# Windowed and global attention feeding a two-layer network: another order of the global columns, the stores and the value products

## The chip, the cores and the metric

The kernel runs on one core of a Trainium2 chip. The metric is the device time of one execution in microseconds (us), median of several runs. A core has five instruction streams that run side by side and meet only at semaphores: TensorE (PE in the profile, with its weight loads as PEld), VectorE (DVE), ScalarE (ACT), GpSimd (POOL) and SyncE (SP), which here only issues DMAs. Each stream executes its instructions in the order in which they stand.

## The reference

For 8 batches and 8 heads of width 64 there are 512 local and 32 global positions. Global queries attend to all 544 positions. Local queries attend to the 32 global keys and to local keys at most 32 positions away. The attention output (4352 rows of 512) then goes through a gated network with 2048 inner columns.

```python
s_g = scale * q_g @ concat(k_g, k_l).T ;  out_g = softmax(s_g) @ concat(v_g, v_l)
s_l = concat(scale * q_l @ k_g.T, where(|i - j| <= 32, scale * q_l @ k_l.T, -1e9))
out_l = softmax(s_l) @ concat(v_g, v_l)
x = concat(out_g, out_l) as rows of 512     # 8 * 544 rows
h = x @ w_in                                # 512 x 2048
out = (h * sigmoid(h)) @ w_out              # 2048 x 512
```

All inputs and the output are float32. The network's products, and from step 28 on the score products, are made out of rounded parts: a value is split into a high part (a cast) and a low part (value minus high part), and a product is a sum of high and low terms.

## The kernel before

**Attention steps.** Work is cut into 128 steps; step k is one batch, one chunk of 128 local queries and one pair of heads, so a batch has 16 steps. A step goes through these functions:

- `st_load` (L295) brings queries and keys, `st_vload` (L303) the values; both DMAs are issued by SP. `st_split` (L311) makes high and low parts for steps from `ND` = 28 on: a ScalarE cast (L317) and two VectorE subtractions (L318, L319).
- `st_scores` (L321): PE products into a PSUM bank `s` (L336), then the softmax: mask and minimum on VectorE (L340), exponential on ScalarE (L344), scaling (L348, L349). The result is `probs`, two buffers.
- For steps from `KF` = 16 on the probabilities are turned by DMA: `st_halves` (L359) copies them on POOL into 16-bit halves, `st_away` (L364) writes these to DRAM, `st_back` (L368) reads them back with a transposing DMA into the tile `pt`. There are three `pt` tiles, used in turn. Steps before 16 are turned by PE (L377).
- `st_turn` (L371) adds the columns of the global queries of the same batch to `pt`: a POOL copy from `pgt` (L386) and, in the last chunk of a batch, one from `pgu` (L389).
- `st_out` (L391): the value products (L403) into a PSUM bank `o`, evacuated to the network's input by ScalarE (L405) and VectorE (L407), with the global part added to `acc` (L413).

**Global steps.** In the course of batch b the global queries of batch b + 1 are prepared, at four steps of the batch, the heads of the stream: `g_load` (L217), `g_split` (L222), `g_scores` (L233), which makes two products `gs`, each evacuated by ScalarE (L247 or L251) and, for batches from 3 on, VectorE (L252), and, after two of them, `g_soft`. The names `gs_4_1` and the like give batch and head pair. The first of the two products goes to a bank of kind `s`, the second to kind `o`. Once the first network block is done, `attbank` (L80) has one single bank for everything of kind `o`, so that a value product that follows a `gs` product has to wait until the `gs` product has been read out. `g_turn` (L273), at the start of a batch, turns the global probabilities and writes `pgt` and `pgu`.

**The network.** It runs in 12 blocks of row tiles (`SIZES`: one tile, then eleven blocks of three). Block n has 16 pairs of `first_layer` (L538: 12 products `h` at L551, then ScalarE L557, VectorE L559, ScalarE L563, VectorE L564) and `second_layer` (L567: for each of three tiles the products L579, L580, L581 into banks `out`). At the end of a block each `out` is evacuated by ScalarE (L590) into one of two buffers and stored by a DMA (L592). In blocks 2 to 10 that DMA keeps its place in program order on SP (`hold`). The weights' high and low parts are made once, in blocks 0 and 1, by `split_weights` (L204): ScalarE casts (L211), POOL subtractions (L212).

**What sets the order.** Attention and network share PE. Every function of a step is put into one list with a due time: a step takes one unit, and each head widens its step by 0.3. The tables `DUE`, `DMAT` (for steps from 16 on), `HEAD` and `TURN` hold the due times relative to the step's start. The list is sorted, and `fill` (L524) emits what is due between two pieces of the network. PE executes exactly in this order. The other engines' order is chosen by a scheduler, except where `hold` keeps program order.

Of the kernel before, what the change touches and what calls it, by code (L numbers as in the profile page):

```python
# [38 lines left out]
SIZES = (1,) + (3,) * 11  # L39
BUFS = dict(qk=2, raw=2, p=2, vraw=4, halves=1, pt=3)  # L40
ND = 28
KF = 16
# [1 line left out]
KP = 12  # L44
SCRATCH = 8
FETCH, LOOK = 4, 2
SPLIT0, SPLITS = 14, 1.0
FIRSTW = {0: 2, 1: 1, 2: 1, 3: 2}

FIRST = dict(load=(-1.2, -1.1, -1.0, 0.1), vload=(-0.9, 0.2, 0.3, 1.1), turn=(3.2, 4.0, 4.9, 5.8), out=(4.3, 5.2, 6.1, 7.0),  # L50
# [1 line left out]
             join=(3.9, 5.0, 5.9, 6.8), late=8.5, then=7.3)  # L52

DUE = dict(load=-1.2, split=-0.5, vload=-0.6, turn=1.6, out=2.2)
DMAT = dict(vload=1.5, halves=0.7, away=1.05, back=1.7, turn=2.3, out=3.0)
HEAD = dict(load=-0.2, split=0.45, scores=0.65, soft=0.85, slot=0.3)
HEADS0, HEADS = (10, 1), (7, 2)
TURN = (1.5, 2.6)
FULL = 0.98
END = 0.5  # L60

# [1 line left out]
def attention_moe_kernel(ctx: ExitStack, tc: tile.TileContext, qk0_in, qk_in, v_in, gqk, wts, out):  # L63
    nc = tc.nc
# [69 lines left out]
    def pt_tile(k):  # L134
        return pts[k % len(pts)]
# [30 lines left out]
    hold = tc.keep_in_program_order  # L166
# [90 lines left out]
    def did(what, *needs):  # L257
        for need in needs:
            assert need in order_done, (what, need)
        order_done.add(what)  # L260
# [32 lines left out]
    tiles = {}  # L293
# [70 lines left out]
        hold(nc.sync.dma_start(out=away, in_=tiles.pop(("halves", k)).rearrange("p h u j -> p h (u j)")))  # L364

    def st_back(k, b, c, pr):
        pt = tiles["pt", k] = pt_tile(k)
        hold(nc.sync.dma_start_transpose(out=pt.bitcast(U16).rearrange("p u a q -> p (u a) q")[:, :, : 2 * P],  # L368
                                         in_=tiles.pop(("away", k)).rearrange("q h j -> (q h) j")))

    def st_turn(k, b, c, pr):  # L371
        if k < KF:
            t = attbank("t", f"t{k}")
            p = tiles.pop(("p", k))
            assert k in held_by.values()
            for i in range(4):
                nc.tensor.transpose(t[:, i * P : (i + 1) * P], p[:, i * P : (i + 1) * P], ident.bitcast(F32))  # L377
            pt = tiles["pt", k] = pt_tile(k)
            nc.scalar.copy(out=pt[:, :, :, :P], in_=t.rearrange("p (u a q) -> p u a q", u=2, a=2))
        else:  # L380
            pt = tiles["pt", k]
        if k < NPR:
            return
        did(("last", b) if (c, pr) == (NC - 1, NPR - 1) else k, ("turn", b, pr // 2))
        pgt, pgu = state["pgt"]
        nc.gpsimd.tensor_copy(out=pt[:, :, 0, P:], in_=pgt[:, c, 2 * pr : 2 * pr + 2, :])  # L386
        if c == NC - 1:
            src = pgu[SG * pr : SG * (pr + 1), :].rearrange("p (u q) -> p u q", u=2)
            nc.gpsimd.tensor_copy(out=pt[:SG, :, 1, P:], in_=src)  # L389
# [65 lines left out]
    at = 0.0  # L455

    def put(when, fn, *a):
        stream.append((when, fn, a))

    AHEAD = NPR  # L460
    for k, (t, b, c, pr) in enumerate(steps):
        a = (k, b, c, pr)
        j = k % NST
        due = dict(DUE)
        if k >= KF:
            due.update(DMAT)
        if k < AHEAD:
            due.update({part: FIRST[part][k] - k for part in ("load", "vload", "turn", "out")})
        if k == AHEAD:
            for h in range(NPR):  # L470
                put(FIRST["gload"][h], g_load, 0, h)
                put(FIRST["gscores"][h], g_scores, 0, h)
                put(FIRST["join"][h], join_weights)
            for hh in range(2):
                put(FIRST["gsoft"][hh], g_soft, 0, hh)
                put(FIRST["gturn"][hh], g_turn, 0, hh)
            put(FIRST["late"], g_late)
            at = FIRST["then"]
        if j == 0 and b:
            for hh in range(2):  # L480
                put(at + TURN[hh], g_turn, b, hh)
        for i in range(FIRSTW.get(k, 0)):
            put(at + 0.01, fetch_weights, nc.sync)
        put(at + due["load"], st_load, *a)
        put(at + due["split"], st_split, *a)
        put(at, st_scores, *a)
        put(at + due["vload"], st_vload, *a)
        if k >= KF:
            put(at + due["halves"], st_halves, *a)
            put(at + due["away"], st_away, *a)  # L490
            put(at + due["back"], st_back, *a)
        put(at + due["turn"], st_turn, *a)
        put(at + due["out"], st_out, *a, t)
        marks[t] = at + due["out"]
        if j == NST - 1 and b % 4 == 3:
            put(marks[t] + 0.001, g_tile, t + 1)
            marks[t + 1] = marks[t] + 0.001
        if b + 1 < B:
            for h in [h for h in range(NPR) if int((HEADS if b else HEADS0)[0] + h * (HEADS if b else HEADS0)[1]) == j]:
                for part, fn in (("load", g_load), ("split", g_split), ("scores", g_scores)):  # L500
                    put(at + HEAD[part], fn, b + 1, h)
                if h % 2:
                    put(at + HEAD["soft"], g_soft, b + 1, h // 2)
                at += HEAD["slot"]
        at += 1.0
# [61 lines left out]
    def second_layer(n, f, gh, gl):  # L567
        if f == 0:
            outs[n] = [ps_out.tile([P, DM], F32, tag=f"out{i}", name=f"out{n}_{i}") for i in range(SIZES[n])]
        wh, wl = (w_hi[f][:, DM:], w_lo[f][:, DM:]) if n else (w_32[2 * f + 1], None)  # L570

        last = n + 1 == len(SIZES) and f == NF - 1
        for i in (reversed(range(SIZES[n])) if last else range(SIZES[n])):
            o = outs[n][i]
            sl = slice(i * P, (i + 1) * P)
            if n == 0:
                nc.tensor.matmul(o, gh[:, sl], wh, start=(f == 0), stop=(f == NF - 1))
            else:
                nc.tensor.matmul(o, gh[:, sl], wh, start=(f == 0), stop=False)  # L579
                nc.tensor.matmul(o, gh[:, sl], wl, start=False, stop=False)  # L580
                nc.tensor.matmul(o, gl[:, sl], wh, start=False, stop=(f == NF - 1))  # L581
            fill(1)
        if f == NF - 1:
            for i in (reversed(range(SIZES[n])) if last else range(SIZES[n])):
                o = outs[n][i]
                if last and i == 0:
                    sb = raws.tile([P, QW + KW], F32, tag="raw", name="o_last")[:, :DM]
                else:
                    sb = two.tile([P, DM], F32, tag="o", name=f"o{n}_{i}")
                nc.scalar.activation(sb, o, AF.Copy, scale=0.5)  # L590
                for p0, np_, r in out_rows(sum(SIZES[:n]) + i):
                    store = nc.sync.dma_start(out=out[r : r + np_, :], in_=sb[p0 : p0 + np_, :])  # L592
                    if 1 < n < len(SIZES) - 1:
                        hold(store)

    advance(ends[0])
    early.clear()
# [1 line left out]
    for n in range(len(SIZES)):  # L599
        for f in range(NF):  # L600
# [13 lines left out]
            if pend is not None:  # L614
                second_layer(*pend)
            pend = (n, f, *g)
    second_layer(*pend)


# [67 lines left out]
```

## Time and profile before

| quantity | value |
|---|---|
| three runs | 1060.27, 1054.97, 1062.12 us; median 1060.27 us |
| profiled execution | 1055.09 us, span from first to last instruction 1053.3 us |
| mean granted TensorE clock | 0.986 of full speed |
| PE busy, of the span | 996.9 us (95%) |
| DVE, ACT, POOL busy | 612.0, 577.9, 233.1 us |
| DMA issues by SP | 112 transposing DMAs `pt<-away`, 40 stores, and the loads |

In a row of the profile, `L403 PE MATMUL o<-pt,vraw` is line, engine, operation, and what is written from what is read, buffer numbers left out. Behind a group of instructions stand busy time and mean nanoseconds of one, then the idle time of the engine just before them with what ended it. In a timeline a row is start, duration, engine and line; in square brackets stands the idle time before it and what ended that. "issue" means that the profile shows no releaser. A PE instruction's end is modelled, and matmuls overlap, so their pace is read from their starts. PEclk is the TensorE clock that was granted.

### The profile page before, as it was taken

The numbers are of one execution on the slowest core, as the hardware profiler recorded it, in microseconds if no ns is written. First come the engines' busy times: TensorE is split into PE (matmuls) and PEld (weight loads), VectorE is DVE, ScalarE is ACT, GpSimd is POOL, SyncE is SP. The second block draws the span as 40 slices with busy tenths as digits, with TensorE's granted clock in tenths as the row PEclk, the third lists the DMA queues.
The fourth block names the chain that finished last, engine by engine and source line by source line (L and its number), as shares of the span: only waits on it lengthen the run. The fifth ranks groups of instructions, "written<-read, shape, count | busy, mean of one in ns | idle before, by whom it ended". The sixth has DMA issues, their size and how long they took to land.

```text
span 1053.3 us, 17559 instructions
## 1 busy us (share of the span) xinstructions
PE 996.9 (95%) x5680; PEld 847.1 (80%) x5680; DVE 612.0 (58%) x1941; ACT 577.9 (55%) x1517; POOL 233.1 (22%) x437
## 2 busy tenths in 40 slices
PE   7898998999989998999998999899989999999997
PEld 5666886888878887888887887788778888888996
DVE  4777544656676666665556665665566657552222
ACT  6687665655555555564455556556555656542322
POOL 2003765222222212211112222112212222110000
PEclk8899999999999999999999999999999999999999
DMA  8795454556565665555446556555645656630000
GB/s 301 273 349 177 116 146 112 157 150 168 143 181 144 156 178 143 148 144 139 118 119 146 145 152 179 140 152 151 172 135 141 163 155 160 165 92 26 30 1 30
DMA packets 185562, 155.23 MB, mean 147 GB/s; under 512 B 125824, under 2 KB 145792, under 8 KB 185472
## 3 DMA queue, kind: packets, MB, share of 16 engines
q1 hardware_dynamic: 181728, 140.49, 48.9%
q10 hardware_dynamic: 3744, 13.63, 3.6%
q8 instruction: 45, 0.74, 0.3%
q14 instruction: 45, 0.37, 0.1%
HBM read 86.44 MB, written 38.27 MB: 118 GB/s over the span
## 4 chain that ended last, share of the span: by engine, by line
PE 79%; DMA 7%; ACT 4%; DVE 4%; issue 3%; POOL 2%; SPq 0%; ACTq 0%; POOLq 0%; DVEq 0%
PE h L551 31%; PE out L579 11%; PE out L581 10%; PE out L580 10%; PE o L403 7%; PE s L336 6%; DMA raw_g<-in_gqk_dram 2%; ACT probs L344 2%; DMA raw<-in_qk_dram 2%; DMA pt<-away 1%; POOL halves L359 1%; DMA away<-halves 1%; PE h L545 1%; DMA vraw<-in_v_dram 1%; PE gs L246 1%
## 5 line engine op out<-in xcount | busy, mean ns | idle before, releaser
L359 POOL COPY halves<-probs 128x512 uint16<-128x512 uint16 x224 | 145.0, 670 | 487.2 <-DVE probs L349 303.1
L551 PE MATMUL h<-xh,w_hi 128*128 128x384 f32 x704 | 239.9, 341 | 0.0
L551 PE MATMUL h<-xh,w_lo 128*128 128x384 f32 x704 | 237.3, 337 | 0.7 <-POOL w_lo L212 0.7
L551 PE MATMUL h<-xl,w_hi 128*128 128x384 f32 x704 | 236.6, 336 | 0.0
L579 PE MATMUL out<-w_hi,gh 128*128 128x512 f32 x528 | 216.1, 409 | 0.7 <-ACT o L590 0.7
L581 PE MATMUL out<-w_hi,gl 128*128 128x512 f32 x528 | 209.7, 397 | 0.6 <-DVE gl L564 0.6
L580 PE MATMUL out<-w_lo,gh 128*128 128x512 f32 x528 | 209.1, 396 | 0.0
L557 ACT ACTIVATE t<-h 128x384 f32<-128x384 f32 (+1 forms) x192 | 90.2, 470 | 192.8 <-PE h L551 189.6
L559 DVE SCALAR_TENSOR_TENSOR t<-t,h 128x384 f32<-128x384 f32 x176 | 97.3, 553 | 149.0 <-ACT t L557 147.3
L344 ACT ACTIVATE probs<-probs,st 128x224 f32<-128x224 f32 x244 | 115.9, 476 | 78.0 <-DVE st L340 76.8
L564 DVE TENSOR_TENSOR gl<-t,gh 128x384 fp32r<-128x384 f32 x176 | 104.9, 596 | 74.4 <-PE out L581 63.6
L551 PEld LDWEIGHTS h<-xh,w_hi 128*128 128x128 f32 x704 | 132.6, 188 | 8.5 <-issue 2.7
L551 PEld LDWEIGHTS h<-xl,w_hi 128*128 128x128 f32 x704 | 132.5, 188 | 6.0 <-issue 0.5
L551 PEld LDWEIGHTS h<-xh,w_lo 128*128 128x128 f32 x704 | 132.2, 188 | 1.4 <-POOL w_lo L212 1.4
L340 DVE CUSTOM_DVE_ANT_0 probs<-s,mask 128x224 f32<-128x224 f32 x244 | 86.0, 388 | 62.9 <-PE s L336 55.2
L403 PE MATMUL o<-pt,vraw 128*64 128x160 f32 (+1 forms) x1024 | 95.3, 303 | 27.5 <-issue 16.2
L563 ACT CAST gh<-t 128x384 fp32r<-128x384 f32 x176 | 89.9, 511 | 55.6 <-DVE t L559 54.6
L403 PEld LDWEIGHTS o<-pt,vraw 128*64 128x64 f32 x1024 | 62.6, 137 | 70.7 <-issue 45.6
L581 PEld LDWEIGHTS out<-w_hi,gl 128*128 128x128 f32 x528 | 100.1, 190 | 23.9 <-DVE gl L564 1.5
L579 PEld LDWEIGHTS out<-w_hi,gh 128*128 128x128 f32 x528 | 100.7, 191 | 22.9 <-issue 6.0
L580 PEld LDWEIGHTS out<-w_lo,gh 128*128 128x128 f32 x528 | 100.8, 191 | 13.2
L317 ACT CAST qk<-raw 128x704 fp32r<-128x704 f32 x100 | 77.5, 775 | 24.2 <-DMA raw<-in_qk_dram 23.8
(97 smaller groups left out, 1165.5 us busy)
## 6 DMA issues: line engine op xcount, KB each, us to landing
raw<-in_qk_dram SPq DMA_DIRECT2D x100, 352.0 KB, 3.4
away<-halves SPq DMA_DIRECT2D x112, 256.0 KB, 2.1
vraw<-in_v_dram SPq DMA_DIRECT2D x128, 128.0 KB, 3.0
raw_w<-in_wts_dram ACTq DMA_DIRECT2D x26, 512.0 KB, 6.3
raw_g<-in_gqk_dram SPq DMA_DIRECT2D x32, 304.0 KB, 3.6
out_dram<-o SPq DMA_DIRECT2D x31, 256.0 KB, 2.0
raw<-in_qk_dram SPq DMA_DIRECT2D x28, 240.0 KB, 4.2
raw_w<-in_wts_dram SPq DMA_DIRECT2D x6, 512.0 KB, 6.8
```

The costliest lines, as they stand in the source:

```text
L340: nc.vector.tensor_tensor_reduce(out=p[:, u, :W], in0=s[:, u * W : (u + 1) * W], in1=mask_of[c], scale=-SCALE, scalar=3.0e38, op0=ALU.add, ...
L344: nc.scalar.activation(p[:, u, :W], p[:, u, :W], AF.Exp, bias=st[:, u : u + 1], scale=-1.0, accum_out=st[:, 2 + u : 3 + u])
L359: nc.gpsimd.tensor_copy(out=halves[:, :, u], in_=p[:, 2 * P * u : 2 * P * (u + 1)].bitcast(U16).rearrange("p (j h) -> p h j", h=2))
L403: nc.tensor.matmul(o[D * u : D * (u + 1), :m], vraw[:, a, u, :], pt[:, u, a, :m], start=(a == 0), stop=(a == 1))
L551: nc.tensor.matmul(h[:, :nt], wt, x[:, c, :nt], start=(i == 0), stop=(i == 3 * NCC - 1))
L557: nc.scalar.activation(t[:, :nt], h[:, :nt], AF.Tanh, scale=0.5)
L559: nc.vector.scalar_tensor_tensor(out=out[:, :nt], in0=t[:, :nt], scalar=1.0, in1=h[:, :nt], op0=ALU.add, op1=ALU.mult)
L563: nc.scalar.copy(out=gh[:, :nt], in_=t[:, :nt])
L564: nc.vector.tensor_tensor(out=gl[:, :nt], in0=t[:, :nt], in1=gh[:, :nt].bitcast(F32), op=ALU.subtract)
L579: nc.tensor.matmul(o, gh[:, sl], wh, start=(f == 0), stop=False)
L580: nc.tensor.matmul(o, gh[:, sl], wl, start=False, stop=False)
L581: nc.tensor.matmul(o, gl[:, sl], wh, start=False, stop=(f == NF - 1))
```

## The change

The due times of steps from 16 on change: the global columns are copied (`turn`) 1.3 units after the step's start instead of 2.3, and are now put ahead of the transposing DMA (`back`, 1.65 instead of 1.7); `st_turn` takes the `pt` tile, `st_back` finds it taken. The value products come 3.4 units after the scores instead of 3.0, the values' load at 2.2 instead of 1.5. At a head the global load comes at -0.6 instead of -0.2, the split at 0.2 instead of 0.45, the scores at 0.8 instead of 0.65, the softmax at 1.0 instead of 0.85. `g_turn` comes at 0.4 and 1.5 (0.65 and 1.5 for batch 1) instead of 1.5 and 2.6. Weight splits are 0.93 instead of 1.0 pieces apart. The stores of blocks 2 to 10 are issued by ScalarE and no longer held in program order.

```diff
-SPLIT0, SPLITS = 14, 1.0
+SPLIT0, SPLITS = 14, 0.93
-DMAT = dict(vload=1.5, halves=0.7, away=1.05, back=1.7, turn=2.3, out=3.0)
-HEAD = dict(load=-0.2, split=0.45, scores=0.65, soft=0.85, slot=0.3)
+DMAT = dict(vload=2.2, halves=0.7, away=1.05, turn=1.3, back=1.65, out=3.4)
+HEAD = dict(load=-0.6, split=0.2, scores=0.8, soft=1.0, slot=0.3)
-TURN = (1.5, 2.6)
+TURN1, TURN = (0.65, 1.5), (0.4, 1.5)
...
     def st_back(k, b, c, pr):
-        pt = tiles["pt", k] = pt_tile(k)
+        pt = tiles["pt", k]
...
         else:
-            pt = tiles["pt", k]
+            pt = tiles["pt", k] = pt_tile(k)
...
-                put(at + TURN[hh], g_turn, b, hh)
+                put(at + (TURN if b > 1 else TURN1)[hh], g_turn, b, hh)
...
+        put(at + due["turn"], st_turn, *a)
+        if k >= KF:
             put(at + due["back"], st_back, *a)
-        put(at + due["turn"], st_turn, *a)
...
-                    store = nc.sync.dma_start(out=out[r : r + np_, :], in_=sb[p0 : p0 + np_, :])
-                    if 1 < n < len(SIZES) - 1:
-                        hold(store)
+                    queue = nc.scalar if 1 < n < len(SIZES) - 1 else nc.sync
+                    queue.dma_start(out=out[r : r + np_, :], in_=sb[p0 : p0 + np_, :])
```

What it does to the instructions of PE, POOL and ScalarE, at three places. In these rows the line numbers of the kernel after are one higher from L491 on (L552 is L551 of before), a number behind a name tells buffers apart, and `x2` means two equal instructions in a row.

**TensorE, batch 3 of the stream, where the third head prepares batch 4** (`gs_4_2` are its products, `o` the value products that follow, `out` and `h` the network's). Before:

```order
L249 MATMUL gs_4_2_4622<-qk_g_2_4612 128x272
L250 MATMUL gs_4_2_4622<-klo_g_2_4613,qk_g_2_4612 128x272
L249 MATMUL gs_4_2_4627<-qk_g_2_4612 128x272
L250 MATMUL gs_4_2_4627<-klo_g_2_4613,qk_g_2_4612 128x272
L579 MATMUL out_2_4291<-w_hi_1343,gh_5_4534 128x512
L580 MATMUL out_2_4291<-w_lo_1344,gh_5_4534 128x512
L581 MATMUL out_2_4291<-w_hi_1343,gl_5_4535 128x512
L403 MATMUL o_4635<-pt_127,vraw_4540 64x160 x2
L403 MATMUL o_4635<-pt_127,vraw_4540 64x128 x2
```

After:

```order
L249 MATMUL gs_4_2_4622<-qk_g_2_4586 128x272
L250 MATMUL gs_4_2_4622<-klo_g_2_4587,qk_g_2_4586 128x272
L249 MATMUL gs_4_2_4627<-qk_g_2_4586 128x272
L250 MATMUL gs_4_2_4627<-klo_g_2_4587,qk_g_2_4586 128x272
L580 MATMUL out_1_4298<-w_hi_1336,gh_5_4543 128x512
L581 MATMUL out_1_4298<-w_lo_1337,gh_5_4543 128x512
L582 MATMUL out_1_4298<-w_hi_1336,gl_5_4544 128x512
L580 MATMUL out_2_4299<-w_hi_1336,gh_5_4543 128x512
L581 MATMUL out_2_4299<-w_lo_1337,gh_5_4543 128x512
L582 MATMUL out_2_4299<-w_hi_1336,gl_5_4544 128x512
L403 MATMUL o_4647<-pt_127,vraw_4552 64x160 x2
L403 MATMUL o_4647<-pt_127,vraw_4552 64x128 x2
```

Where three `out` products stood between the global scores and the value products, six stand now. The piece between them grows at all 20 heads of batches 3 to 7.

**POOL, about step 27** (`w_lo` are low parts of weights, `w_1051` and `w_1055` the last two weight tiles, `pt_127` to `pt_129` the three tiles `pt`). Before:

```order
L359 COPY halves_1946<-probs_117 128x2x256 x2
L212 TENSOR_TENSOR w_lo_1904<-w_1012,w_hi_1903 128x512 x2
L386 COPY pt_129<-pgt_1133 128x2x32
L212 TENSOR_TENSOR w_lo_1968<-w_1051,w_hi_1967 128x512
L212 TENSOR_TENSOR w_lo_1968<-w_1055,w_hi_1967 128x512
```

After:

```order
L359 COPY halves_1937<-probs_117 128x2x256 x2
L389 COPY pt_129<-pgu_1092 32x2x32
L386 COPY pt_128<-pgt_1091 128x2x32
L212 TENSOR_TENSOR w_lo_1905<-w_1012,w_hi_1904 128x512 x2
L212 TENSOR_TENSOR w_lo_1911<-w_1051,w_hi_1910 128x512
L212 TENSOR_TENSOR w_lo_1911<-w_1055,w_hi_1910 128x512
```

The copy into `pt_128` now belongs to step 28 and stands ahead of the last two pairs of low parts; it may start once the value products of step 25, the tile's last user, are done. Before, the copy in this place was that of step 26, whose tile had been free since step 23.

**ScalarE, the end of network block 6** (`o_0`, `o_1`, `o_2` are the buffers of its three output tiles, `pg` and `gs_6_0` belong to a head). Before:

```order
L590 ACTIVATE o_1_7113<-out_1_6136 128x512
L344 ACTIVATE probs_117,st_7087<-probs_117,st_7087 128x224
L348 ACTIVATE probs_117<-probs_117,st_7087 128x224
L557 ACTIVATE t_1_7132<-h_1_7119 128x384
L251 COPY pg_125<-gs_6_0_7146 64x272
L251 COPY pg_125<-gs_6_0_7151 64x272
L317 CAST qk_7166<-raw_7101 128x704
L563 CAST gh_1_7133<-t_1_7132 128x384
L590 ACTIVATE o_2_7116<-out_2_6137 128x512
```

After:

```order
L594 DMA out_dram<-o_0_7117 32x512 x2
L348 ACTIVATE probs_117<-probs_117,st_7073 128x224
L594 DMA out_dram<-o_0_7117 32x512 x2
L591 ACTIVATE o_1_7123<-out_1_6142 128x512
L317 CAST qk_7159<-raw_7084 128x704
L558 ACTIVATE t_1_7142<-h_1_7129 128x384
L251 COPY pg_125<-gs_6_0_7149 64x272
L594 DMA out_dram<-o_1_7123 128x512
L591 ACTIVATE o_2_7126<-out_2_6143 128x512
L251 COPY pg_125<-gs_6_0_7154 64x272
```

Five store issues and the last two evacuations now stand ahead of the second copy of the global scores, which stood ahead of the last evacuation before.

## The prediction

> **What bounds the kernel now.** First the table of busy times, then two 50 us windows of PE: one without a head that stalls, one with (columns: us, PE busy and its matmuls, PEld, DVE, ACT, POOL, PE clock, DMA share, GB/s).
>
> ```profile
> PE 996.9 (95%) x5680; PEld 847.1 (80%) x5680; DVE 612.0 (58%) x1941; ACT 577.9 (55%) x1517; POOL 233.1 (22%) x437
> 450.00:500.00 50.00, 50.00 (x291) 43.38 (x290) 27.82 (x87) 27.30 (x72) 8.99 (x21) 1.00 0.54 139
> 650.00:700.00 50.00, 43.92 (x249) 38.37 (x248) 33.54 (x106) 27.87 (x71) 9.80 (x21) 0.97 0.56 149
> ```
>
> PE is the bound, and no product is added or removed. The gain can only come from the 56 us in which PE idles, and from time at a lower clock. Next, what ended PE's waits (total us, times, longest), and the group of the value products:
>
> ```profile
> PE o L403 <- issue: 16.2, 11, 3.6
> PE o L403 <- POOL halves L359: 6.7, 5, 1.5
> PE s L336 <- DVE klo L318: 3.5, 1, 3.5
> PE o L403 <- POOL pt L389: 3.0, 3, 1.1
> PE gs L249 <- DVE qk_g L230: 2.9, 3, 1.4
> PE o L403 <- PE h L551: 0.9, 1, 0.9
> PE out L579 <- ACT o L590: 0.7, 2, 0.4
> L403 PE MATMUL o<-pt,vraw 128*64 128x160 f32 (+1 forms) x1024 | 95.3, 303 | 27.5 <-issue 16.2 <-POOL halves L359 6.7 <-POOL pt L389 3.0
> ```
>
> The largest item, 27.5 us ahead of the value products, has three names, and I believe none of them: "issue" says that no releaser was seen. The timeline of a long and of a short one (start, duration, engine, line):
>
> ```profile
> 394.52 0.29 PE L250 MATMUL gs<-klo_g,qk_g 128*128 128x272 f32 x1
> 395.45 0.38 ACT L251 COPY pg<-gs 64x272 f32<-64x272 f32 x1
> 395.85 0.78 ACT L317 CAST qk<-raw 128x704 fp32r<-128x704 f32 x1
> ...
> 396.65 0.38 ACT L251 COPY pg<-gs 64x272 f32<-64x272 f32 x1
> 396.66 0.63 DVE L318 TENSOR_TENSOR klo<-raw,qk 128x448 fp32r<-128x448 f32 x1 [0.19 <-ACT qk L317]
> ...
> 397.64 0.43 DVE L252 TENSOR_TENSOR pg<-gs,pg 64x272 f32<-64x272 f32 x1
> 398.18 0.71 PE L403 MATMUL o<-pt,vraw 128*64 128x160 f32 x8 [3.36 <-issue]
> 427.14 0.29 PE L250 MATMUL gs<-klo_g,qk_g 128*128 128x272 f32 x1
> ...
> 427.63 0.78 DVE L252 TENSOR_TENSOR pg<-gs,pg 64x272 f32<-64x272 f32 x2 [0.27 <-ACT pg L251]
> 428.51 0.36 PE L403 MATMUL o<-pt,vraw 128*64 128x160 f32 x2 [1.08 <-POOL pt L389]
> ```
>
> The second `gs` product sits in the one bank of kind `o`. Two L251 and two L252 read it out, and `o` begins 0.11 us after the last L252 ends (398.18 against 397.64 + 0.43; 428.51 against 427.63 + 0.78). This holds at all 22 such waits from 168 us on, and they sum to 25.6 us. So a gap is *latency + 0.1 − D*: latency from the end of the last `gs` product to the end of the last L252, D the PE work ordered between. At 427 the latency is 0.98 us (428.41 − 427.43), at 394 it is 3.26 (398.07 − 394.81), because a step's cast stands between the two L251 and its subtractions ahead of the last L252. Of the 20 heads of batches 3 to 7, eleven take 0.98 to 1.30 us, four about 2.0 to 2.1, five 2.7 to 3.5.
>
> The gaps have a second price, the clock. Windows of 3.41 us on PE (us, PE busy and matmuls, clock, DMA share, GB/s):
>
> ```profile
> 396.44:399.85 3.41, 1.67 (x13) 1.00 0.70 223
> 553.44:556.85 3.41, 1.25 (x12) 1.00 0.70 180
> 556.85:560.26 3.41, 3.41 (x12) 0.50 0.90 221
> 655.84:659.25 3.41, 0.24 (x2) 1.00 0.55 127
> 659.25:662.66 3.41, 2.98 (x12) 0.50 0.92 181
> 778.72:782.13 3.41, 1.47 (x12) 1.00 0.90 253
> 782.13:785.54 3.41, 3.41 (x10) 0.50 0.57 136
> ```
>
> Three windows at half clock follow windows with 1.47 us of PE work or less; 1.67 leaves the clock whole. Each costs 3.41 × 0.5 = 1.7 us.
>
> **The change part by part,** against the profiled execution: 1055.09 us, of which the span is 1053.3.
>
> *Value products 3.4 steps behind, heads' scores later.* The paces for D:
>
> ```profile
> 960.06 0.34 PE L551 MATMUL h<-xl,w_hi 128*128 128x384 f32 x1
> 960.24 0.34 PE L551 MATMUL h<-xh,w_lo 128*128 128x384 f32 x1
> 962.46 0.40 PE L581 MATMUL out<-w_hi,gl 128*128 128x512 f32 x1
> 962.69 0.39 PE L579 MATMUL out<-w_hi,gh 128*128 128x512 f32 x1
> ```
>
> An `h` product costs 0.174 us over its run of twelve, an `out` product 0.23. At `gs_4_2` three `out` become six: D goes from 0.69 to 1.39. Counted so from the order, D of the heads 3_0 to 7_3 goes from 0.69, 2.09, 0, 0.69 | 1.39, 0, 0.69, 0 | 1.39, 0.69, 0, 0.69 | 1.39, 0, 0.69, 0 | 2.08, 0, 0, 2.09 to 3.91, 2.78, 2.78, 1.39 | 1.82, 2.78, 1.39, 0.69 | 5.29, 1.39, 2.78, 1.39 | 1.82, 2.78, 1.39, 0.69 | 2.51, 2.09, 2.78, 2.78. With each head's own latency of before, what remains is 3_1 0.28, 3_3 0.85, 4_1 0.58, 4_2 0.70, 4_3 0.39, 5_3 0.85, 6_1 0.82, 6_2 0.70, 6_3 0.39, 7_1 0.75, 7_3 0.11: 6.4 us. The two gaps at 168 and 190 (1.3 us) keep 0.1. Saved: 25.6 − 6.5 = **19.1**. The latencies will not stay, since ScalarE's and VectorE's orders change; all at 1.3 us leave 1.4 us, all at 3.0 us leave 19.8. So the term lies between 5.7 and 24.
>
> *The clock.* The windows ahead of 556.85, 659.25 and 782.13 hold the gaps of heads 5_2, 6_1 and 7_1; with D = 2.78, 2.78 and 2.09 they hold at most 0.8 us of idle: **+5.1** (0 to 5.1). The Trainium skill ("TensorE: Matmul & The Clock Gate", Part 1: The HAM clock gate) has the clock fall after an idle window of about 3.4 us. By that rule only the 655.84 window would count and this term would be 1.7 us; the trace speaks against it, with 1.25 and 1.47 us of work in windows that were followed by half clock.
>
> *Global load and split sooner.* The three waits for `qk_g` (2.9 us) go, as split to scores grows from 0.2 to 0.6 units and load to split from 0.65 to 0.8: **+2.9** (0 to 2.9).
>
> *Stores by ScalarE.* SP's long waits and what an issue costs:
>
> ```profile
> SPq L592 <- ACT o L590: 143.4, 23, 62.2
> L592 SPq DMA_DIRECT2D out_dram<-o x39: 332/344/437, 101.9 to 1049.3; - x39
> L177 ACTq DMA_DIRECT2D raw_w<-in_wts_dram x26: 334/430/2464, 27.0 to 82.9; - x26
> L590 ACT ACTIVATE o<-out 128x512 f32<-128x512 f32 x33 | 19.4, 592 | 6.3 <-PE out L581 4.3 <-DMA out_dram<-o 1.9
> ```
>
> SP stood 143.4 us at the stores with later steps' loads and transposes behind. Almost all was covered: one `o` wait, 0.9 us at 749, I put down to it, and 0.7 us of `out` waiting for L590. **+1.6** (0 to 1.6). In exchange 30 issues of 0.344 to 0.43 us stand on ScalarE, 10.3 to 12.9 us; behind them queue the evacuations, exponentials and `h` activations. ScalarE is 55% busy, so I count those that a head's read-out follows: three at the end of block 3 and five at the end of block 6, 8 × 0.43: **−3.5** (0 to −12.9).
>
> *Global columns ahead of the back transpose.* The copy into `pt` of step k now waits for `o` of step k − 3, and POOL's halves and low parts queue behind it.
>
> ```profile
> 178.16 0.56 PE L336 MATMUL s<-klo,qk 128*128 128x224 f32 x1 [3.45 <-DVE klo L318]
> L212 POOL TENSOR_TENSOR w_lo<-w,w_hi x32: 1267/1286/1716, 93.6 to 173.1; 128x512 fp32r<-128x512 f32 x32
> L386 POOL COPY pt<-pgt 128x64 f32<-128x64 f32 x124 | 35.2, 285 | 232.1 <-DMA pt<-away 144.2 <-PE o L403 52.0 <-ACT pgt L285 23.3
> L318 DVE TENSOR_TENSOR klo<-raw,qk 128x448 fp32r<-128x448 f32 x100 | 66.5, 666 | 33.5 <-ACT qk L317 32.4
> ```
>
> At step 28 the product of the first `klo` already waits 3.45 us, for buffers that the last low parts free. After, that chain starts only at `o` of step 25: copy 0.285, three L212 of 1.29, L318 0.67 and handovers of about 0.4, 5.2 us, with about 1 us of PE work (three `out`, one score product) beside it: a 4.2 us wait, **−0.75** (+3.5 if the chain's start is early, −2.5 if L212 takes its 1.72). For the other low parts of blocks 0 and 1 I count nothing: PE's `h L551 <- POOL w_lo` wait is not among the large ones, and between `o` of k − 3 and the first product of a low part I count 3 to 8 us of PE work more than POOL needs. If that cover goes, it is the third rival. Afterwards POOL is free (22% busy), and its 144.2 us wait for the transpose only changes its releaser.
>
> *The rest.* The value load at 2.2 still leaves 1.2 units ahead of 3.4 (1.5 before); `g_turn` sooner and weight pieces 0.93 apart move work within covers: 0.
>
> Sum: 19.1 + 5.1 + 2.9 + 1.6 − 3.5 − 0.75 = 24.5 us, so 1055.1 − 24.5 = 1030.6 for the profiled execution. The median of the three runs stands 5.2 us above that execution; I take half of it as lasting: **1033 us**.
>
> **The rivals.**
>
> 1. *The read-out stays late.* In the order after, casts and subtractions stand ahead of L251 and L252 at more heads. At 3.0 us everywhere 19.8 us remain: +13.4, 1046 us. Against it: eleven of 20 are short now, and longer D meets them.
> 2. *ScalarE pays in full.* All 30 issues delay PE: +9.4, 1042; together with the first rival 1055, within 1% of before. For it: ScalarE's L344 and L557 sit in every chain. Here I also put that the change does not do what it says, the gaps staying whatever D is; against that speaks the formula's agreement at 22 places.
> 3. *Slower: POOL tied to the value products while weights are split.* From 93.6 to 173.1 us POOL makes 32 low parts, in 16 pairs; a copy that stands ahead of them holds each pair until `o` of k − 3 is done. It decides when the chain falls behind by more than the 3 us of cover. Then each pair costs about one L212 (1.29), 21 us, and some ten windows fall to half clock, 17 us: 38 in all, 1071 us. For it: step 28 already waits, and the PE clock is lower in that stretch. Against: POOL is not saturated there.
> 4. *The clock falls for another reason.* If only the window with 0.24 us of work is tied to its gap, two half-clock windows stay: +3.4, 1036 us. That is also what the skill's clock rule would give, as weighed above.
>
> **How the numbers follow.** Forecast 0.54 (own range 1023 to 1041: read-out latencies shorter or longer by a half, ScalarE 0 to −8); better 0.08 (all read-outs short, no cost on ScalarE: 1055 − 24 − 5.1 − 2.9 − 1.6 = 1021, with the run offset some 1019 to 1024); rival 1 0.13; rival 4 0.05; rival 2 0.12; rival 3 0.08. About 1% can be told from no change, so faster means below 1049.7 us: 0.54 + 0.08 + 0.13 + 0.05 = 0.80. Same 0.12, slower 0.08. From 1018 to 1050 the range leaves out rivals 2 and 3, 0.20.
>
> **What would show it.** Right: the idle time ahead of L403 falls from 27.5 to about 8 us; no half-clock window after 200 us; `gs L249 <- qk_g` gone; the store waits gone from SP; a wait of 3 to 5 us at step 28's `klo`. Rival 1 shows as L403 still idle by 15 us or more with L317 between the two L251; rival 2 as PE waits behind L344, L348 or L557 at block ends; rival 3 as `h` waiting for `w_lo` and low clock between 90 and 180 us; rival 4 as half clock in windows that follow busy ones. A wait for the back transpose, which SP now issues behind a POOL copy, would be a cost that I have not counted.

## The result and the profile after

The kernel after takes 1027.45 us (median; 1025.85 to 1028.82), the kernel before beside it 1058.14 us (1054.97 to 1062.12). The ratio is 0.9708, interval 0.9667 to 0.9748: 30.7 us less. The forecast was 1033 us in a range of 1018 to 1050. The profiled execution went from 1055.09 to 1028.82 us, a fall of 26.3 us, of which the forecast's sum had 24.5.

The table of busy times of the kernel after:

```profile
PE 991.6 (97%) x5680; PEld 844.4 (82%) x5680; DVE 612.8 (60%) x1941; ACT 575.2 (56%) x1517; POOL 237.8 (23%) x437
```

PE's waits (total us, times, longest; line numbers are one higher from L491 on):

```profile
PE h L546 <- DVE w L201: 6.9, 4, 2.2
PE o L403 <- issue: 6.5, 10, 1.1
PE s L336 <- DVE klo L318: 4.7, 1, 4.7
PE gt L284 <- ACT pt L379: 1.5, 1, 1.5
PE gu L287 <- DVE st L340: 1.1, 1, 1.1
```

The group of the value products (busy us, mean ns, idle us ahead and what ended it):

```profile
L403 PE MATMUL o<-pt,vraw 128*64 128x160 f32 (+1 forms) x1024 | 96.3, 303 | 7.0 <-issue 6.5 <-ACT pg L247 0.2
```

The span fell by 1053.3 − 1027.0 = 26.3 us. PE's time outside work fell from 56.4 to 1027.0 − 991.6 = 35.4 us, and its busy time by 5.3 us, though the products are the same: less of it runs at half clock. The idle time ahead of L403 carries nearly all of the first part, 27.5 to 7.0 us. The waits for `qk_g` and for `w_lo` are gone. Four small ones grew: `klo` by 1.2, `w` (the first weights, 5.6 us before) by 1.3, and `gt` and `gu`, the turns of the global probabilities, together by 2.1 us.

A head of the kernel after, batch 4's second, which before waited 3.36 us (timeline: start, duration, engine, line):

```profile
390.50 0.29 PE L250 MATMUL gs<-klo_g,qk_g 128*128 128x272 f32 x1
390.90 0.67 ACT L251 COPY pg<-gs 64x272 f32<-64x272 f32 x2
391.48 0.43 DVE L252 TENSOR_TENSOR pg<-gs,pg 64x272 f32<-64x272 f32 x1
392.53 0.43 DVE L252 TENSOR_TENSOR pg<-gs,pg 64x272 f32<-64x272 f32 x1
393.52 0.71 PE L403 MATMUL o<-pt,vraw 128*64 128x160 f32 x8
```

The read-out still takes 2.2 us (392.53 + 0.43 against the end of the last product at 390.79), but three `out` and twelve `h` products lie beside it, and `o` begins 0.56 us after the bank is free with no idle time noted. The same reckoning over the twenty heads of batches 3 to 7 leaves 4.8 us of gaps, the longest 1.15 us.

The clock (us, PE busy and matmuls, clock, DMA share, GB/s), around step 28 of the kernel after:

```profile
173.59:177.01 3.42, 0.04 (x1) 1.00 0.82 190
177.01:180.43 3.42, 2.08 (x6) 0.50 0.10 40
180.43:183.84 3.41, 3.41 (x12) 0.50 0.00 0
```

Two windows in a row are at half clock here, where before it was one. From there to the last microseconds none is: the windows of before at 557, 659 and 782 us are gone. Between 20 us and the last microseconds before had six windows at half clock (two from 38 us, one at 178), and after has three (one at 71 us, and these two).

### The profile page after: what moved, and what is told of

It is laid out like the page before. It is cut to its first block, busy times and chain, and to the rows that moved or that the text cites. A ratio compares the mean times of both kernels' runs of the same rounds, so it can differ in the third digit from the quotient of the medians.

```text
span 1027.0 us, 17590 instructions
## 1 busy us (share of the span) xinstructions
PE 991.6 (97%) x5680; PEld 844.4 (82%) x5680; DVE 612.8 (60%) x1941; ACT 575.2 (56%) x1517; POOL 237.8 (23%) x437
## 4 chain that ended last, share of the span: by engine, by line
PE 86%; DMA 5%; ACT 3%; DVE 2%; issue 1%; POOL 0%; SPq 0%; ACTq 0%; DVEq 0%; POOLq 0%
PE h L552 35%; PE out L580 13%; PE out L582 11%; PE out L581 11%; PE o L403 7%; PE s L336 5%; DMA raw_w<-in_wts_dram 3%; DMA raw<-in_qk_dram 1%; ACT w L198 1%; PE gt L284 1%; DMA raw_g<-in_gqk_dram 1%; PE out L578 1%; PE h L546 1%; PE gs L246 1%; PE gs L250 0%
## 5 line engine op out<-in xcount | busy, mean ns | idle before, releaser
L552 PE MATMUL h<-xh,w_hi 128*128 128x384 f32 x704 | 241.7, 343 | 0.0
L552 PE MATMUL h<-xh,w_lo 128*128 128x384 f32 x704 | 237.4, 337 | 0.0
L552 PE MATMUL h<-xl,w_hi 128*128 128x384 f32 x704 | 237.0, 337 | 0.0
L359 POOL COPY halves<-probs 128x512 uint16<-128x512 uint16 x224 | 148.5, 687 | 205.1 <-issue 89.1
L552 PEld LDWEIGHTS h<-xh,w_hi 128*128 128x128 f32 x704 | 132.8, 189 | 11.2 <-issue 5.2
L386 POOL COPY pt<-pgt 128x64 f32<-128x64 f32 x124 | 33.1, 268 | 456.0 <-PE o L403 358.8
L552 PEld LDWEIGHTS h<-xl,w_hi 128*128 128x128 f32 x704 | 132.8, 189 | 6.1 <-issue 0.5
L552 PEld LDWEIGHTS h<-xh,w_lo 128*128 128x128 f32 x704 | 132.6, 188 | 0.0
L403 PE MATMUL o<-pt,vraw 128*64 128x160 f32 (+1 forms) x1024 | 96.3, 303 | 7.0 <-issue 6.5
L403 PEld LDWEIGHTS o<-pt,vraw 128*64 128x64 f32 x1024 | 62.9, 137 | 47.0 <-issue 43.3
```

The lines of the kernel that those rows point to most:

```text
L359: nc.gpsimd.tensor_copy(out=halves[:, :, u], in_=p[:, 2 * P * u : 2 * P * (u + 1)].bitcast(U16).rearrange("p (j h) -> p h j", h=2))
L403: nc.tensor.matmul(o[D * u : D * (u + 1), :m], vraw[:, a, u, :], pt[:, u, a, :m], start=(a == 0), stop=(a == 1))
L552: nc.tensor.matmul(h[:, :nt], wt, x[:, c, :nt], start=(i == 0), stop=(i == 3 * NCC - 1))
```

## The experiments

Each is a kernel of its own, timed beside the kernel before. e1 to e4 ran on one chip, e5 to e8 on a second, e9 to e11 on a third.

**Only the distance of the value products (e1).** On the kernel before:

```diff
             due.update(DMAT)
+        if k >= 36:
+            due["out"] = 3.4
```

> The kernel before, with only the value products moved: 3.4 units behind the scores from step 36 on (3.0 in the steps before). Counted from the order, the PE work D between a head's second gs product and the value product behind it grows from a mean of 0.73 us to 3.20 us. Theory (the gaps are the read-out latency minus D, in one bank): idle ahead of L403 falls from 27.5 us to 3 to 8 us, the half-clock windows near 557, 659 and 782 us go, and the time is 1028 to 1037 us, 21 to 30 us below before. The waits for qk_g (2.9 us) and for klo at step 28 (3.5 us) stay. Rival (the gain comes from the stores leaving SP, or from the global columns' place): 1050 us or more, L403 still idle by over 15 us.

Measured: 1030.45 us, ratio 0.9745 (0.9723 to 0.9766). The group of the value products:

```profile
L403 PE MATMUL o<-pt,vraw 128*64 128x160 f32 (+1 forms) x1024 | 94.4, 301 | 4.7 <-issue 1.6 <-POOL pt L386 1.4 <-POOL halves L359 0.8
```

The idle time falls to 4.7 us and there is no half-clock window from 20 us to the tail. The profile is of an execution of 1024.83 us at a granted clock of 0.995; the other four took 1029.5 to 1030.7 us at 0.990 to 0.993, so the median may hold such windows. One number of the change, alone, brings 26 us where the whole brings 31. The waits for `qk_g`, expected to stay at 2.9, fell to 0.8.

**Another bank, same order (e2).** On the kernel before:

```diff
-            s = attbank(kind, f"gs{j}_{b}_{p}")
+            s = attbank(kind if b < GF else "s", f"gs{j}_{b}_{p}")
```

> The kernel before, with one edit: from batch 3 on a head's second gs product goes to a bank of kind s as the first does, not to the single bank of kind o. D stays 0.73 us on average. Theory (the value product waits for the bank alone): the gaps of batches 3 to 7 (24.3 us) go whatever D is, with them the three half-clock windows (5.1 us): 1026 to 1034 us. A part may come back as waits of score products for the bank that gs now holds. Rival (the value products wait for something else at that time, the global columns or the halves that the profile names): the gaps stay and the time is that of before, 1053 to 1063 us.

Measured: 1027.38 us, ratio 0.9718 (0.9688 to 0.9749). The group of the value products:

```profile
L403 PE MATMUL o<-pt,vraw 128*64 128x160 f32 (+1 forms) x1024 | 95.3, 303 | 3.1 <-issue 1.1 <-POOL halves L359 0.8 <-ACT pt L379 0.7
```

The same head of batch 4 in the timeline:

```profile
390.05 0.29 PE L250 MATMUL gs<-klo_g,qk_g 128*128 128x272 f32 x1
390.27 0.71 PE L403 MATMUL o<-pt,vraw 128*64 128x160 f32 x8
391.80 0.38 ACT L251 COPY pg<-gs 64x272 f32<-64x272 f32 x1
392.21 0.78 ACT L317 CAST qk<-raw 128x704 fp32r<-128x704 f32 x1
...
393.01 0.38 ACT L251 COPY pg<-gs 64x272 f32<-64x272 f32 x1
...
394.00 0.43 DVE L252 TENSOR_TENSOR pg<-gs,pg 64x272 f32<-64x272 f32 x1
```

The read-out is as late as before, with the cast between the two L251, and ends at 394.43. The value products start at 390.27, right behind the `gs` product. All twenty gaps behind the heads of batches 3 to 7 are gone; the 0.8 us that still go by "POOL halves" are ahead of the value product at 169 us, behind a head of batch 2, which e2 leaves in its place. What the twenty waited for was the bank and nothing else; "POOL halves" and "POOL pt" in the profile of before were names of bystanders.

**Stores on SP again (e3).** On the kernel after:

```diff
-                    queue = nc.scalar if 1 < n < len(SIZES) - 1 else nc.sync
-                    queue.dma_start(...)
+                    store = nc.sync.dma_start(...)
+                    if 1 < n < len(SIZES) - 1:
+                        hold(store)
```

> The kernel after, with the stores of blocks 2 to 10 issued by SP again and held in program order. Theory (the stores are worth about nothing: at most 1.6 us of waits come back, at most 3.5 us of ScalarE's issue time go): 1023 to 1031 us, no verdict against the kernel after's 1027.5. Rival (the change's gain is SP's 143 us of waits at the stores): 1045 us or more.

Measured: 1033.89 us, ratio 0.9779 (0.9761 to 0.9797), against 0.9710 for the kernel after (e5): between the two theories. The end of block 2 in the timeline:

```profile
287.75 6.94 SPq L593 DMA_DIRECT2D out_dram<-o  x3
292.36 0.67 ACT L251 COPY pg<-gs 64x272 f32<-64x272 f32 x2
292.93 0.78 ACT L317 CAST qk<-raw 128x704 fp32r<-128x704 f32 x1
293.74 0.60 ACT L591 ACTIVATE o<-out 128x512 f32<-128x512 f32 x1
294.38 0.50 PE L580 MATMUL out<-w_hi,gh 128*128 128x512 f32 x1 [1.82 <-ACT o L591]
```

Windows of PE there:

```profile
291.60:295.01 3.41, 1.59 (x10) 1.00 0.02 6
295.01:298.43 3.42, 3.42 (x12) 0.50 0.99 248
```

With the stores on SP, ScalarE's third read-out L591 stands behind a head's copies and a cast; in e5 it stands ahead of them, at 290.02 us. PE waits 1.82 us for it, and the window that holds the wait is followed by one at half clock, 1.7 us more. In this profile these are 3.5 of the 5.5 us of span that separate it from the kernel after in e5 (1031.4 against 1025.9). The rest is a balance of smaller differences; the idle time ahead of L403 goes the other way, 5.0 against 8.1 us. SP's three stores took 6.94 us, as it stood waiting for that read-out.

**Copies behind the transposing DMA again (e4).** On the kernel after:

```diff
-DMAT = dict(vload=2.2, halves=0.7, away=1.05, turn=1.3, back=1.65, out=3.4)
+DMAT = dict(vload=2.2, halves=0.7, away=1.05, back=1.7, turn=2.3, out=3.4)
-TURN1, TURN = (0.65, 1.5), (0.4, 1.5)
+TURN1, TURN = (1.5, 2.6), (1.5, 2.6)
...
(st_back takes the pt tile, and is put ahead of st_turn, as before)
```

> The kernel after, with the global columns copied behind the transposing DMA again (copy at 2.3, DMA at 1.7, the tile taken by the DMA) and the turns of the global probabilities at 1.5 and 2.6 as before. D is that of the kernel after. Theory (this part is worth nothing but the wait at step 28): 1023 to 1030 us, the wait for klo at step 28 at about 3.5 us where it is 4.7 now. Rival (the copy ahead of the DMA is what lets the value products come early): 1040 us or more, with L403 waiting for the copy L386 or L389 or for the DMA.

Measured: 1028.87 us, ratio 0.9724 (0.97 to 0.9748), no different from the kernel after (0.9667 to 0.9748). So this part, the turns of the global probabilities with it, is worth nothing that can be measured; the waits of `gt` and `gu` are gone. The wait at step 28 did not go back to 3.5 us (timeline):

```profile
171.08 5.04 POOL L212 TENSOR_TENSOR w_lo<-w,w_hi 128x512 fp32r<-128x512 f32 x4
174.93 1.67 DVE L318 TENSOR_TENSOR klo<-raw,qk 128x448 fp32r<-128x448 f32 x1 [3.96 <-POOL w_lo L212]
...
176.65 0.55 PE L336 MATMUL s<-klo,qk 128*128 128x224 f32 x1 [5.81 <-DVE klo L318]
```

Here no copy that waits for `o` stands ahead of the four L212, and still the wait is 5.81 us. They begin 1.7 us sooner than in the kernel after (171.08 against 172.76), but PE's first score product of step 28 starts 2.8 us sooner (170.57 against 173.37). What sets the wait is when the last four L212 begin against PE's order, and the copy is only one of the things that can come ahead of them.

In the kernel before, the wait of 3.45 us had another cause (timeline):

```profile
171.89 2.86 POOL L212 TENSOR_TENSOR w_lo<-w,w_hi 128x512 fp32r<-128x512 f32 x2 [0.48 <-ACT w_hi L211]
177.03 0.42 DVE L319 TENSOR_TENSOR qk<-raw,qk 64x256 fp32r<-64x256 f32 x1 [1.26 <-ACT qk L317]
177.48 1.16 DVE L318 TENSOR_TENSOR klo<-raw,qk 128x448 fp32r<-128x448 f32 x2
```

The last L212 ends at 174.75 us, when PE's wait has just begun. The first `klo` starts 2.7 us later, because on VectorE both L318 stand behind step 29's L319, and that waits for ScalarE's cast.

**The kernel after beside e6 to e8 (e5),** unchanged.

> The kernel after, unchanged, beside the next three for a comparison on one chip: 1024 to 1031 us, 0.967 to 0.975 of before.

Measured: 1027.25 us, ratio 0.9710 (0.9681 to 0.9739).

**Only the stores (e6).** On the kernel before:

```diff
-                    store = nc.sync.dma_start(...)
-                    if 1 < n < len(SIZES) - 1:
-                        hold(store)
+                    queue = nc.scalar if 1 < n < len(SIZES) - 1 else nc.sync
+                    queue.dma_start(...)
```

> The kernel before, with only the stores of blocks 2 to 10 issued by ScalarE and not held. D stays 0.73 us on average, so the gaps ahead of L403 stay at 22 to 28 us in both theories. Theory (30 issues of 0.34 us on ScalarE cost little, and SP's store waits cost 1.6 us and what block ends wait for read-outs): 1050 to 1058 us. Rival (the stores cost or bring as much as the value products): below 1047 or above 1062 us.

Measured: 1045.23 us, ratio 0.9883 (0.9853 to 0.9913): 12.5 us less, which is the rival's case. The table of busy times:

```profile
PE 990.4 (95%) x5680; PEld 842.5 (81%) x5680; DVE 610.8 (59%) x1941; ACT 578.1 (55%) x1517; POOL 234.0 (22%) x437
```

The group of the value products:

```profile
L403 PE MATMUL o<-pt,vraw 128*64 128x160 f32 (+1 forms) x1024 | 95.1, 302 | 26.5 <-issue 10.9 <-POOL halves L359 6.7 <-POOL pt L386 5.2
```

The head at 394 us in the timeline:

```profile
395.10 0.38 ACT L251 COPY pg<-gs 64x272 f32<-64x272 f32 x1
395.40 0.78 DVE L252 TENSOR_TENSOR pg<-gs,pg 64x272 f32<-64x272 f32 x2
395.92 0.77 ACT L317 CAST qk<-raw 128x704 fp32r<-128x704 f32 x1
396.29 0.71 PE L403 MATMUL o<-pt,vraw 128*64 128x160 f32 x8 [1.53 <-issue]
```

The sum of the gaps hardly moves (27.5 to 26.5), as both theories had it. But their sizes do. ScalarE's order came out otherwise, the cast no longer splits the two L251, and the two gaps of over 3 us are now 1.53 each; the longest ahead of a value product is 2.8 us. PE's busy time falls by 6.5 us, and the three half-clock windows after 500 us, 5.1 us, are gone. So 6.5 of the 10.4 us of span are busy time, most of it clock, and 3.9 are idle time. The largest part of the idle time is the waits for `qk_g`, 2.9 to 0.7 us. In the kernel before, two of those three waits (0.73 and 1.42 us) come from the stores. The longer one in the timeline of before:

```profile
545.17 3.06 SPq L592 DMA_DIRECT2D out_dram<-o  x3
548.32 0.38 SPq L219 DMA_DIRECT2D raw_g<-in_gqk_dram  x1
552.37 0.70 ACT L228 CAST qk_g<-raw_g 128x608 fp32r<-128x608 f32 x1 [1.43 <-DMA raw_g<-in_gqk_dram]
554.52 0.36 PE L249 MATMUL gs<-qk_g 128*128 128x272 f32 x1 [1.42 <-DVE qk_g L230]
```

SP issues the head's global load right behind the three stores of the block's end, 6.2 us ahead of the product that needs it. In e6 it does so 15.3 us ahead of that product, which starts at 551.03 us without a wait:

```profile
535.69 0.52 SPq L219 DMA_DIRECT2D raw_g<-in_gqk_dram  x1
```

The three windows went in three ways. The window ahead of 557 held 1.08 us of this `qk_g` wait and a gap of 1.08 us ahead of L403; the wait went, while the gap grew to 1.40. The one ahead of 659 lost its gap of 3.60 us to one of 1.53. The one ahead of 782 went by very little: its gap is still 2.78 us (2.84 before), and the window holds 1.53 us of work where it held 1.47:

```profile
767.57:770.99 3.42, 1.53 (x10) 1.00 0.60 146
770.99:774.40 3.41, 2.52 (x16) 1.00 0.86 209
```

**The heads' old times (e7).** On the kernel after:

```diff
-HEAD = dict(load=-0.6, split=0.2, scores=0.8, soft=1.0, slot=0.3)
+HEAD = dict(load=-0.2, split=0.45, scores=0.65, soft=0.85, slot=0.3)
```

> The kernel after, with the head's load, split, scores and softmax at the old times (-0.2, 0.45, 0.65, 0.85). Counted from the order D is 3.27 us on average (2.3 in the kernel after). Theory: the gaps ahead of L403 fall from 7.0 to 3 to 5 us, waits for qk_g of 1 to 3 us come back, the sum within 3 us of the kernel after. Rival (loading and splitting the global queries sooner carries part of the gain): 5 us or more above the kernel after.

Measured: 1023.79 us, ratio 0.9681 (0.9647 to 0.9716), 3.5 us below the kernel after on the same chip, with no overlap of their runs (1021.0 to 1024.9, 1026.2 to 1028.0). The gaps fell as expected; the group of the value products:

```profile
L403 PE MATMUL o<-pt,vraw 128*64 128x160 f32 (+1 forms) x1024 | 94.9, 302 | 4.8 <-issue 4.0 <-ACT pt L379 0.7
```

No wait for `qk_g` came back, and the wait for `w` fell from 7.1 us in e5 to 4.8. The head's new times are the part of the change that costs. They move the scores 0.15 units nearer to the value products behind them (in e5 the idle time ahead of L403 is 8.1 us), and the first weights are waited for longer.

**Value products at 3.0 (e8).** On the kernel after:

```diff
-DMAT = dict(vload=2.2, halves=0.7, away=1.05, turn=1.3, back=1.65, out=3.4)
+DMAT = dict(vload=2.2, halves=0.7, away=1.05, turn=1.3, back=1.65, out=3.0)
```

> The kernel after, with the value products 3.0 units behind the scores as before. Against the heads' scores at 0.8 this puts D at 5.1 us on average, since the value product of the same step now falls ahead of the gs products and the next one follows a step later. Theory (only where the value products lie against the heads counts, not how far behind the scores): gaps ahead of L403 1 to 4 us, 1021 to 1029 us, at or below the kernel after. Rival (the longer distance is needed so that the turned probabilities and the copies on POOL are there): L403 waits for the transposing DMA or L386, 4 us or more above the kernel after.

Measured: 1037.0 us, ratio 0.981 (0.9771 to 0.9849), 10 us above the kernel after. Neither theory's account holds: L403 waits no longer (5.7 us), and not for the DMA. PE's largest wait:

```profile
PE gs L249 <- DVE acc L413: 11.2, 12, 2.2
```

One head in the timeline:

```profile
565.95 0.71 PE L403 MATMUL o<-pt,vraw 128*64 128x160 f32 x8
566.82 0.29 PE L250 MATMUL gs<-klo_g,qk_g 128*128 128x272 f32 x1
...
568.95 0.18 DVE L413 TENSOR_TENSOR acc<-o,acc 128x32 f32<-128x32 f32 x1
569.27 0.56 PE L249 MATMUL gs<-qk_g 128*128 128x272 f32 x1 [2.16 <-DVE acc L413]
```

It is the same bank, seen from the other side. The value products now stand right ahead of the `gs` products, and the second `gs` product waits until VectorE has read `o` out, 12 times and 11.2 us in all. Three windows fall to half clock as well. D must be large on both sides of the `gs` product; my count looked only behind it.

**Old heads and another bank (e9).** On e7:

```diff
-        s = attbank(kind, f"gs{j}_{b}_{p}")
+        s = attbank(kind if b < GF else "s", f"gs{j}_{b}_{p}")
```

> The kernel after with the heads' old times and, from batch 3 on, the second gs product in a bank of kind s. D is 3.27 us on average, but the value product no longer shares a bank with it. Theory: the gaps left behind heads with the old times (one of 2.1 us with a half-clock window behind it, one of 0.8 us) go: 4 to 5 us off, 1017 to 1022 us. Rival (the distance has already taken all, or the s banks are now waited for): no gain, 1022 to 1028 us.

Measured: 1020.65 us, ratio 0.9662 (0.9648 to 0.9676), the lowest median of all. The idle time ahead of L403 is 3.2 us, and none of it is behind a head of batches 3 to 7; from 200 us to the last microseconds no window is at half clock. By the ratios it beats the kernel after by about 5 us. What the bank adds to e7 (0.9681) is not shown in the time, since the two intervals overlap.

**Early value products nearer (e10).** On e7:

```diff
             due.update(DMAT)
+        if KF <= k < 30:
+            due["out"] = 3.0
```

> The kernel after with the heads' old times and the value products of steps 16 to 29 at 3.0 instead of 3.4. Only the copy into the tile of step 28 comes free sooner, and with it the last low parts on POOL. Theory: the wait for klo at step 28 falls from 3.7 to about 1.6 us and the half-clock window near 174 us may go: 1019 to 1024 us. Rival (the wait is set by POOL's own rate in that stretch): 3.5 us stay, 1022 to 1027 us.

Measured: 1024.84 us, ratio 0.9705 (0.9689 to 0.9721). The wait at step 28 fell to 1.9 us, but no time was gained against e7 (0.9681), where 1019 to 1024 us were expected: a head of batch 2 at 170 us now has the value product close behind it, which waits 2.5 us for the read-out by L247.

**Scores sooner (e11).** On e10:

```diff
-HEAD = dict(load=-0.2, split=0.45, scores=0.65, soft=0.85, slot=0.3)
+HEAD = dict(load=-0.4, split=0.2, scores=0.5, soft=0.7, slot=0.3)
```

> The kernel after with the heads' scores at 0.5 (load -0.4, split 0.2, softmax 0.7) and the value products of steps 16 to 29 at 3.0. Counted from the order D is 3.9 us on average and nowhere below 2.08. Theory: gaps ahead of L403 behind the heads at most 1 us in all, no half-clock window after 200 us: 1016 to 1022 us. Rival (scores put that early wait for the split, as 0.3 units lie between): waits for qk_g of 3 us or more, 1022 us or more.

Measured: 1023.79 us, ratio 0.9692 (0.9678 to 0.9707), above the 1016 to 1022 us expected. Behind the heads of batches 3 to 7 nothing is left, as D said, and no window after 200 us is at half clock. The head at 170 us took it back (timeline):

```profile
167.20 2.16 ACT L211 CAST w_hi<-w 128x512 fp32r<-128x512 f32 x4
169.65 0.65 ACT L247 COPY pg<-gs 64x272 f32<-64x272 f32 x2
170.35 0.72 PE L403 MATMUL o<-pt,vraw 128*64 128x160 f32 x8 [3.31 <-ACT pg L247]
```

Four casts of weights stand ahead of its read-out. Batch 2 was outside my count of D, which took batches 3 to 7.

## Why the prediction was right, and where not

- **The formula.** "A gap is latency + 0.1 − D", in one bank: shown from both sides. e1 changes D and the gaps follow; e2 takes the bank away, keeps D, and the gaps vanish with the read-out as late as ever. In the kernel after, 20.5 us of idle time ahead of L403 went, where the term had 19.1. The count of 22 places is 21, since the head at 762 us did not wait. The latencies did change, but the two read-outs of about 2.7 us met a D of 2.8 and 3.9, which nothing in the forecast made sure of; the first rival did not come.
- **What makes D large.** The term's heading named the value products at 3.4 and the heads' scores later as one cause. They work against each other: with 3.4 alone in place of both, D is 3.27 instead of 2.27 us (e7), and the time is 3.5 us lower. A later score is right only with value products at a distance that leaves room on both sides (e8).
- **The clock, +5.1.** The three windows went, and one was added behind the longer wait at step 28; ahead of that, two became one. So three windows fewer, 5.1 us, and PE's busy time fell by 5.3 us in all. But these windows were not the distance's alone. Half of the idle time in the window ahead of 557 was a wait for `qk_g`, not a gap of a head as the forecast had it, and the stores by themselves (e6) take all three away too. They can be won once, which is one reason why 26 and 12.5 us apart make 31 together; the waits for `qk_g` are another.
- **`qk_g`, +2.9.** Right in size, wrong in cause. The step was "split to scores grows". With the old head times the wait stays away (e7). Two of the three waits, 2.15 of the 2.9 us, came from a load that SP could issue only behind the three stores of a block's end. The stores alone (e6) take these two away. So does the distance alone (e1), where the two loads stand ahead of the stores. What caused the third, 0.72 us at 761 us, is open.
- **The stores, +1.6 − 3.5.** This is the term that was wrong. Alone they are worth 12.5 us, and on top of the rest 6 to 7 (e3 against e5: 0.9779 and 0.9710). I counted PE's waits that I could put down to SP and the cost of the issues on ScalarE. "Almost all was covered" is the step that failed: behind the stores stood global loads that PE then waited for, 2.15 us of `qk_g` and half of the idle time ahead of the half clock at 557 us. I also left out that ScalarE's and VectorE's order is chosen anew when a held instruction goes, which sets both the read-outs of `gs` and those of `out`. How the 12.5 us divide between the two is not shown, and the clock's share holds some luck (the window with 1.53 us of work). The 3.5 us of cost did not show: no PE wait of the kernel after ends on a store's issue, and the second rival did not come. The Trainium skill ("DMA: Bandwidth & Descriptors", Issuing engines are not separate DMA queues) says that another issuing engine saves only the time to initiate a DMA. The runs here go beyond that: the issue costs 0.34 us on ScalarE, and what was saved is SP's wait for data, 6.94 us at one block end of e3.
- **Step 28, −0.75.** The wait was forecast at 4.2 us and is 4.72; POOL's copy waits for `o` and the four L212 follow, as the step had it. The half-clock window behind it (1.7 us) was not counted. That the copy is the one cause fell with e4, where the wait is 5.81 us without it. The reading of before was wrong: the low parts were done 2.7 us ahead of the first `klo`, which waited for its turn on VectorE.
- **POOL tied to the value products, 0.** Right: `w_lo` no longer holds PE at all, and the third rival had no place. e4 shows the whole part to be worth nothing that can be measured.
- **"The rest", 0.** `g_turn` sooner cost 2.1 us at `gt` and `gu` in this execution and 1.2 in e5's of the same kernel; e4, with the old times, has neither wait. I had named no cover for it. The wait for `w`, 1.3 us more, goes with the heads' new times: 6.9 to 7.1 us in all five runs that have them, 4.8 to 5.7 in the others. The value load at 2.2 and the weight pieces at 0.93 were not tested alone.
- **The chances.** The second rival alone was priced at 1042 us, inside the range and below the bound for "faster", and yet its 0.12 went to "same". The result did not put this to the test.

The sum fits better than its terms, in part by luck. Read by waits, the fall of 26.3 us is 20.5 ahead of L403, 5.3 of busy time, 2.9 for `qk_g` and 1.4 for `out` and `w_lo`, less 1.2 for `klo`, 2.1 for `gt` and `gu` and 1.3 for `w`, with small ones left over. The 3.5 us of cost on ScalarE, which did not come, cancel against the last two, which were not counted. Read by the parts of the change it is further off: on top of the rest the stores are worth 6 to 7 us where the sum had -1.9, and the heads' new times, credited with `qk_g`, cost 3.5.

## What to carry to other kernels

Where two streams share one bank, the read-out of each must fit into the work ordered before the other's next use, on both sides; count that work from the order, against the read-out's duration from the timeline. A bank for each does the same without any count. When an instruction that is held in order is taken off a queue, look first at what stood behind it on that queue and who waited for that; then expect the scheduler to move other engines' work, and look for gain or loss there.

## What the runs showed of the hardware

The clock falls behind a window that is not idle. Over the thirteen profiles, windows of 3.41 us counted from the edges of the clock's record, at full clock, without the first and the last 20 us of the span: all 23 with less than 1.5 us of PE work (44% of the window) were followed by half clock, none of those with 1.8 us or more, and of the 18 between 1.5 and 1.8 seven were. One of that zone that was followed by half clock, from e8:

```profile
309.68:313.09 3.41, 1.79 (x15) 1.00 0.00 0
313.09:316.51 3.42, 3.42 (x13) 0.50 0.81 246
```

The window of e6 with 1.53 us, shown above, was not followed by it.

So idle time of somewhat more than half a window is enough, and so was every gap of 2 us that fell whole into one window. That the sum counts and not one long gap rests on a single window, the one at 553.44 us of before, where no gap is longer than 1.08 us. What decides between 1.5 and 1.8 us stays open; PE's ends in the trace are modelled, and an error of 0.1 us or two could make that zone. This bears out the prediction's reading against the rule of the Trainium skill ("TensorE: Matmul & The Clock Gate", Part 1: The HAM clock gate) that it takes an idle window.
